# ScalarE loads the projection, TensorE multiplies zeros meanwhile, GpSimd copies the query maxima, and a new order table

## The chip, the cores and the metric

The kernel runs on one core of a Trainium2 chip. A core has five engines that run side by side, each through its own list of instructions in order: TensorE (PE, matrix products), VectorE (DVE), ScalarE (ACT), GpSimd (POOL) and SyncE (SP, which here only issues DMA transfers). The metric is the device time of one launch in microseconds; a kernel's time is the median of its runs.

## The reference

Two stages follow each other. The first is a linear attention with positive features for 8 batches and 8 heads of 576 tokens with 64 values each; the second is a feed-forward layer with a cosine gate.

```
def phi(x):                                        # 64 -> 256 features
    proj = einsum('bhsd,df->bhsf', x, w_phi)       # w_phi: 64 x 128
    proj = proj - max(abs(proj), axis=-1)
    return concatenate([exp(proj), exp(-proj)])
kv  = einsum('bhsf,bhsd->bhfd', phi(k), v);  z = sum(phi(k), axis=2)
out = (phi(q) @ kv) / (phi(q) @ z + 1e-6)          # -> x, 4608 tokens x 512
h = x @ w_in;  g = h * cos(h);  y = g @ w_out      # 512 -> 2048 -> 512
```

## The kernel before

The attention goes by 32 units of two heads each (`attention(u)`, L427). A unit's queries are projected by `q_mm` (L451) in two halves with the features on the partitions, copied out by ScalarE (`q_copy`, L457), and reduced to the largest absolute value over 128 features in three moves on VectorE: `q_red` (L464) reduces inside quarters of 32 partitions, `q_max` (L470) takes the maximum of the four quarters and writes it into each of the four (L474 once, L476 four times), `q_turn` (L478) transposes it so that GpSimd can subtract it (`q_sub`, L482). Keys are projected by `k_mm` (k_mm and a small k_end) with the tokens on the partitions; `k_max` takes their maxima on VectorE, and for the first eight units `k_sub` subtracts them by a matmul. ScalarE's `exp_k` and `exp_q` follow, then `kv_mm`, `z_mm` and `n_mm` on TensorE, the division (`invert`, `spread`, `turn`, `times`) and the store to `xs`.

The feed-forward layer goes by chunks of 512 tokens and by 16 tiles of the hidden width; `course` lists 15 visits of a chunk to some of the tiles (`visit(v)`). A visit runs `mm1`, a cosine on ScalarE and VectorE, and `mm2` (written as four steps "one" for a visit's first tile). The weights arrive as 64-bit words and are converted once (`convert(ft)`, L353): for the first four tiles GpSimd does three of the moves (`w.rest`, `w.low`, `w.add`), for the others VectorE.

Every piece of work is a `Step` with an engine, a cost, what it depends on and the buffers that it takes; the steps are numbered in the order in which the code makes them. The order in which they are issued is not computed: the table `ORDER` (L86) lists all 2888 numbers. An engine's instruction list is the table cut down to that engine's steps, so a late step holds up all that stands behind it on its engine. `plan()` (L240) walks the table, keeps a clock from the written costs, and gives each step that takes a bank of PSUM the bank that this clock says is free first.

Before all steps stand the constants: SyncE issues `w_phi` twice into the halves of `wphi` (L309), which all projections read; GpSimd writes small constants. The matrix products have four array shapes: full (mm1, mm2, one, k_sub, k_end), upper (q_mm, k_mm: 64 rows), left (kv_mm, n_mm: 64 columns) and quarter (z_mm: 32 columns).

Of the kernel before, what the change touches and what calls it, by code (L numbers as in the profile page):

```python
# [25 lines left out]
def phi_attention_then_cos_ffn(ctx: ExitStack, tc: tile.TileContext, qT, kT, vS, vT, w_phi, w_in, w_out, out):  # L26
# [41 lines left out]
    class Step:  # L68
# [15 lines left out]
    SWITCH = dict(e=1.3, s=1.3, full=0.21, left=0.145, quarter=0.12, upper=0.2)  # L84
    SHAPE = dict(mm1="full", mm2="full", one="full", k_mm="upper", k_end="full", t_mm="upper", t_end="full", s_mm="full", k_sub="full", kv_mm="left", n_mm="left", z_mm="quarter", q_mm="upper")
    ORDER = [  # L86
# [151 lines left out]
    LATENCY = dict(PE=0.35, ACT=0.25, DVE=0.2, POOL=0.25, SP=2.2)  # L238

    def plan():  # L240
        free = dict.fromkeys(LATENCY, 0.0)
        free["port"] = 0.0
        table = {}
        last = {}
# [702 lines left out]
```

## Time and profile before

| | us |
|---|---|
| median of 3 runs (lowest, highest) | 1092.85 (1092.62, 1094.83) |
| profiled execution | 1094.05 |
| its span in the trace | 1092.3 |
| TensorE busy / its weight loads | 1075.4 / 827.7 |
| VectorE busy | 725.2 |
| ScalarE busy | 717.2 |
| GpSimd busy | 127.3 |

Times inside a trace count from the start of its span. An engine's busy time leaves out the instructions of its sequencer. Matmuls are pipelined: each shows longer than the distance to its successor.

### The profile page before, as it was taken

The page shows a single profiled execution, that of the slowest core. Times are in us where ns is not written, and L with a number is a line of the kernel's source. Part 1 is how long each engine was busy: PE and PEld are TensorE (multiplying, and loading weights), DVE is VectorE, ACT ScalarE, POOL GpSimd, SP SyncE. Part 2 cuts the span into 40 slices and gives each one's busy share as a digit, 9 for nine tenths or more (in the row PEclk, how much of TensorE's full clock was granted, in tenths as well). Part 3 has the DMA queues.
Part 4 walks back from the last instruction along what each step waited for, and adds up shares of the span by engine and source line. Part 5 has one row for each costly group of instructions (what it writes and reads, how often), then busy time and mean ns, then how long its engine had stood idle before and what let it go on. Part 6 is the DMA issues. An engine that isn't in the chain of part 4 may idle for free.

```text
span 1092.3 us, 19509 instructions
## 1 busy us (share of the span) xinstructions
PE 1075.4 (98%) x7664; PEld 827.7 (76%) x7664; DVE 725.2 (66%) x1298; ACT 717.2 (66%) x1386; POOL 127.3 (12%) x91
## 2 busy tenths in 40 slices
PE   7999999999999999999999999999999999999998
PEld 4656666778888887788677787787777778888886
DVE  5899999989889868555577366773665354343432
ACT  5888889977666587657567666857667654443533
POOL 2654221000000011101031011110111000000000
PEclk9999999999999999999999999999999999999999
DMA  6564664356667355555241651345211620630441
GB/s 193 150 192 121 193 193 142 97 167 208 224 203 242 109 196 159 195 180 222 55 149 69 205 185 46 106 176 192 93 61 61 250 99 2 222 125 20 146 191 48
DMA packets 92603, 160.71 MB, mean 147 GB/s; under 512 B 43744, under 2 KB 52064, under 8 KB 84320
## 3 DMA queue, kind: packets, MB, share of 16 engines
q1 hardware_dynamic: 92512, 159.48, 43.9%
q8 instruction: 60, 0.98, 0.4%
q14 instruction: 31, 0.25, 0.1%
HBM read 117.51 MB, written 41.94 MB: 146 GB/s over the span
## 4 chain that ended last, share of the span: by engine, by line
PE 86%; DVE 6%; issue 0%; DMA 0%; ACT 0%; DVEq 0%
PE bank L798 35%; PE bank L832 12%; PE bank L833 12%; PE bank L834 12%; PE bank L691 4%; PE bank L642 4%; PE bank L681 2%; PE bank L455 2%; PE bank L493 2%; PE bank L648 1%; PE bank L568 0%; DVE g_c__1102 L809 0%; DMA out<-o_last 0%; DVE m_u__975 L466 0%; DVE g_c__1972 L809 0%
## 5 line engine op out<-in xcount | busy, mean ns | idle before, releaser
L813 ACT ACT_TABLE_LOAD x22 | 28.2, 1283 | 0.4
L484 POOL TENSOR_TENSOR pq_u__3673<-pq_u__3673,bq_u__4170 128x576 f32<-128x576 f32 x2 | 3.6, 1796 | 186.1 <-DVE bq_u__4170 L480 186.1
L872 DVE TENSOR_TENSOR o<-bank,o 128x512 f32<-128x512 f32 x24 | 16.2, 679 | 0.7 <-DMA o<-sums 0.5
L881 DVE COPY o<-bank 128x512 f32<-128x512 f32 x16 | 10.8, 677 | 5.9 <-PE bank L834 4.7
L603 ACT ACT_TABLE_LOAD x11 | 14.1, 1283 | 0.2
L879 ACT ACTIVATE o<-bank 128x512 f32<-128x512 f32 x16 | 9.5, 593 | 5.5 <-PE bank L834 5.5
L598 ACT ACT_TABLE_LOAD x10 | 12.8, 1283 | 0.2
L798 PE MATMUL bank<-xh_c__7472,w 128*128 128x512 f32 x32 | 12.8, 400 | 0.0
L798 PE MATMUL bank<-xh_c__6688,w 128*128 128x512 f32 x32 | 12.8, 399 | 0.0
L798 PE MATMUL bank<-xh_c__5272,w 128*128 128x512 f32 x32 | 12.8, 399 | 0.0
L798 PE MATMUL bank<-xh_c__4458,w 128*128 128x512 f32 x32 | 12.7, 396 | 0.0
L798 PE MATMUL bank<-xh_c__7041,w 128*128 128x512 f32 x32 | 12.5, 390 | 0.0
L798 PE MATMUL bank<-xh_c__5868,w 128*128 128x512 f32 x32 | 12.5, 390 | 0.0
L798 PE MATMUL bank<-xh_c__8219,w 128*128 128x512 f32 x32 | 12.5, 390 | 0.0
L798 PE MATMUL bank<-xh_c__5790,w 128*128 128x512 f32 x32 | 12.5, 390 | 0.0
L798 PE MATMUL bank<-xh_c__7889,w 128*128 128x512 f32 x32 | 12.5, 390 | 0.0
L798 PE MATMUL bank<-xh_c__6645,w 128*128 128x512 f32 x32 | 12.5, 390 | 0.0
L798 PE MATMUL bank<-xh_c__5941,w 128*128 128x512 f32 x32 | 12.5, 390 | 0.0
L798 PE MATMUL bank<-xh_c__4514,w 128*128 128x512 f32 x32 | 12.5, 390 | 0.0
L798 PE MATMUL bank<-xh_c__4696,w 128*128 128x512 f32 x32 | 12.5, 390 | 0.0
L798 PE MATMUL bank<-xh_c__7074,w 128*128 128x512 f32 x32 | 12.5, 390 | 0.0
L798 PE MATMUL bank<-xh_c__8223,w 128*128 128x512 f32 x32 | 12.5, 390 | 0.0
(3837 smaller groups left out, 4061.7 us busy)
## 6 DMA issues: line engine op xcount, KB each, us to landing
w<-w_parts SPq DMA_DIRECT2D x48, 1024.0 KB, 5.0
w_parts<-w SPq DMA_DIRECT2D x16, 1024.0 KB, 5.5
vmain<-vS SPq DMA_DIRECT2D x32, 256.0 KB, 4.7
out<-o SPq DMA_DIRECT2D x32, 256.0 KB, 3.0
sums<-o SPq DMA_DIRECT2D x24, 256.0 KB, 3.3
o<-sums SPq DMA_DIRECT2D x24, 256.0 KB, 3.2
vtail<-vT SPq DMA_DIRECT2D x64, 16.0 KB, 3.7
out<-o_last SPq DMA_DIRECT2D x4, 256.0 KB, 2.0
```

Of the source, the lines that this page charges most:

```text
L455: PE.matmul(out=ps[j], lhsT=wphi[r, :], rhs=d["qr"][r, hf * HALF:(hf + 1) * HALF], start=True, stop=True)
L493: PE.matmul(out=ps[j][:, P * s:P * s + P], lhsT=x[r, P * s:P * s + P], rhs=wphi[r, :], start=(s == 0), stop=w, skip_group_check=True)
L603: ACT.activation(out=e[:, s, :], in_=d["pq"][:, j * S:(j + 1) * S], func=AF.Exp, scale=1.0 - 2.0 * s)
L642: PE.matmul(out=acc[c:c + 64, n, i, :], lhsT=e[:, s, P * n + c:P * n + c + 64], rhs=vmain[u % 2][:, s, i, :], start=(s == 0 and i == 0 and ...
L681: PE.matmul(out=ps[32 * g:32 * g + 32], lhsT=d["z"][:, 2 * n + j, :], rhs=d["eq", j][:, n, hf * HALF:(hf + 1) * HALF], start=(n == 0), sto ...
L691: PE.matmul(out=d["nps", hf][64 * j:64 * j + 64], lhsT=d["kv"][:, 2 * n + j, :], rhs=d["eq", j][:, n, cut[hf]], start=(n == 0 and hf == 0) ...
L798: PE.matmul(out=h, lhsT=a[:, cs], rhs=d[b, kt], start=(k == 0), stop=(k == 3 * KT - 1))
L813: ACT.activation(out=m["g"], in_=m["g"], func=AF.Sin, bias=halfpi, scale=1.0)
L832: PE.matmul(out=a, lhsT=gh[:, t], rhs=w[:, 0], start=first, stop=False)
L833: PE.matmul(out=a, lhsT=gh[:, t], rhs=w[:, 1], start=False, stop=False)
L834: PE.matmul(out=a, lhsT=gl[:, t], rhs=w[:, 0], start=False, stop=last)
L872: DVE.tensor_tensor(out=o, in0=bank(acc[tb]), in1=o, op=ALU.add)
```

## The change

ScalarE's queue issues the two loads of `wphi`. VectorE writes a 128x128 tile of zeros, and TensorE multiplies it with itself seven times into bank 7 ahead of all steps. `q_max` writes the maxima into the first quarter only, and a new step `q_spread` copies them to the other three on GpSimd; `q_turn` depends on it. `plan()` no longer keeps a clock: a step gets the bank whose last user stands earliest in the table. The table is a new one, for 2920 steps (one more per unit). The written costs and latencies also differ, but in the new kernel nothing reads them any more.

```diff
     ORDER = [
-        0, 41, 2, 5, 3, 6, 7, 4, 8, 10, 11, 43, 46, 16, 57, 9, 12, 1192, 18, 20, 13, 44, 45, 48, 61, 19, 17, 58, 21,
...
-        2724, 2819, 2823, 2824, 2825, 2830, 2838, 2839, 2831, 2811, 2832, 2833, 2845, 2803, 2812, 2826, 2840, 2820,
...
+        2914, 2916, 2918, 2917, 2915, 2919,
     ]
...
     def plan():
-        free = dict.fromkeys(LATENCY, 0.0)
...
+        place = {steps[x]: i for i, x in enumerate(ORDER)}
+        owner = [None] * len(banks)
+
+        def last(b):
+            return -1 if b is None else max(place[v] for v in b.users)
 
         for x in (steps[i] for i in ORDER):
...
             for b in x.take:
                 if b.ring == "bank":
-                    at, b.slot = empty(x.eng)
+                    b.slot = min(range(len(banks)), key=lambda i: last(owner[i]))
+                    assert last(owner[b.slot]) < place[x]
                     owner[b.slot] = b
...
     for j in range(2):
-        SP.dma_start(out=wphi[64 * j:64 * j + 64, :], in_=w_phi)
+        ACT.dma_start(out=wphi[64 * j:64 * j + 64, :], in_=w_phi)
     halfpi = const.tile([P, 1], F32, name="halfpi")
     POOL.memset(halfpi, PI_2)
+
+    warm = const.tile([P, P], F32, name="warm")
+    DVE.memset(warm, 0.0)
...
+    WARM = 7
...
             DVE.tensor_tensor(out=m2, in0=m1[0:64], in1=m1[64:128], op=ALU.max)
-            for i in range(4):
-                DVE.tensor_tensor(out=m3[32 * i:32 * i + 32], in0=m2[0:32], in1=m2[32:64], op=ALU.max)
+            DVE.tensor_tensor(out=m3[0:32], in0=m2[0:32], in1=m2[32:64], op=ALU.max)
+
+        def q_spread():
+            m3 = d["m3"]
+            for i in range(1, 4):
+                POOL.tensor_copy(out=m3[32 * i:32 * i + 32], in_=m3[0:32])
...
-            qm = Step("DVE", 0.94, q_max, reds, take=[b["bq"]], use=[b["pq"]], port=True, kind=phase + "q_max")
-            qm = Step("DVE", 1.4, q_turn, [qm], use=[b["bq"]], kind=phase + "q_turn")
+            qm = Step("DVE", 0.41, q_max, reds, take=[b["bq"]], use=[b["pq"]], port=True, kind=phase + "q_max")
+            qm = Step("POOL", 0.45, q_spread, [qm], use=[b["bq"]], port=True, kind=phase + "q_spread")
+            qm = Step("DVE", 1.3, q_turn, [qm], use=[b["bq"]], kind=phase + "q_turn")
...
     with tc.manual_schedule(engines={ENG.PE, ENG.Activation, ENG.DVE, ENG.Pool, ENG.SP}):
+        for _ in range(WARM):
+            PE.matmul(out=banks[7][:, 0:P], lhsT=warm, rhs=warm, start=True, stop=True, skip_group_check=True)
         for x in plan():
             x.fn()
```

Cut down to TensorE's steps (a number is the unit, or with v the visit), the two tables begin like this:

```
before: q_mm0 x2, q_mm1 x2, k_mm0, k_mm1, k_sub0, k_end0, k_end1, k_sub0, k_sub1 x2, k_sub0, kv_mm0 x3, k_end2, k_sub1, k_mm2, ...
after:  k_mm0, q_mm0 x2, q_mm1 x2, k_sub0, k_end0, k_sub0, k_end1, k_sub0, k_mm1, kv_mm0 x3, k_sub1 x3, k_mm2, q_mm2, z_mm0, ...
```

SyncE's list begins with load0, load1, w.load0, load_v0, load2, load3, w.load1 before, and with load0, load1, load_v0, w.load0, load2, load_v1, load3 after.

## Rows read from the trace of the kernel before

**Rows 1.** The page's slices: busy tenths of 40 equal parts of the span.

```profile
PE   7999999999999999999999999999999999999998
...
DVE  5899999989889868555577366773665354343432
```

**Rows 2.** Stretches: length, busy us (and instructions) by engine, clock, DMA share, GB/s.

```profile
12.80:200.00 187.20, 181.16 (x2066) 118.77 (x2063) 175.43 (x349) 160.15 (x354) 72.79 (x42) 1.00 0.52 160
200.00:1080.00 880.00, 879.97 (x5534) 697.86 (x5534) 544.79 (x938) 551.50 (x1023) 53.13 (x34) 1.00 0.42 144
```

**Rows 3.** TensorE's waits from 12.8 to 200 us: total, times, longest; nine rows.

```profile
PE bank L590 <- DVE mk_u__293 L580: 1.6, 1, 1.6
...
PE bank L455 <- DVE pk_u__1718 L585: 0.2, 1, 0.2
```

**Rows 4.** Timeline of TensorE: start, length, instruction; the fourth visit's first matmul.

```profile
239.75 0.39 PE L798 MATMUL bank<-xh_c__2680,w 128*128 128x512 f32 x1
```

**Rows 5.** The chain that ended last: start, length, what; around 262 and 570 us.

```profile
261.68 5.44 PE bank L798 x24
...
562.72 5.47 PE bank L798 x24
568.19 1.11 PE bank L681 x16
569.29 2.10 PE bank L691 x16
571.39 1.87 PE bank L642 x64
...
573.71 0.69 PE bank L455 x4
574.39 0.89 PE bank L493 x16
575.28 0.49 PE bank L455 x4
```

**Rows 6.** Timeline of the first 14 us, with idle time before and its releaser.

```profile
0.81 1.21 SPq L309 DMA_DIRECT2D wphi<-w_phi  x2
...
1.68 0.52 POOL L325 MEMSET vtail<- 64x1 f32 x4
...
5.27 2.29 PE L455 MATMUL bank<-qr_u__117,wphi 64*128 64x288 f32 x8 [5.27 <-DMA qr_u__117<-qT]
...
7.05 0.48 DVE L466 TRANSPOSE_TENSOR_REDUCE m_u__129<-pq_u__130 128x9 f32<-128x288 f32 x1 [7.05 <-ACT pq_u__130 L462]
...
10.75 1.92 PE L493 MATMUL bank<-wphi,kr_u__118 64*128 64x128 f32 x16
...
12.46 1.20 PE L493 MATMUL bank<-wphi,kr_u__122 64*128 64x128 f32 x16
...
12.70 0.69 DVE L580 TENSOR_REDUCE mk_u__169<-bank 128x4 f32<-128x512 f32 x1 [2.38 <-PE bank L493]
```

**Rows 7.** DMA issues of the first 14 us: median us from issue to landing.

```profile
kr_u__118<-kT SPq DMA_DIRECT2D x1, 320.0 KB, 3.4
...
qr_u__121<-qT SPq DMA_DIRECT2D x1, 288.0 KB, 5.5
```

**Rows 8.** Line L476: ns min/median/max, first and last start; units 0, 1 and 5.

```profile
L476 DVE TENSOR_TENSOR m_u__160<-m_u__159 x4: 184/186/189, 9.5 to 10.1; 32x36 f32<-32x36 f32 x4
L476 DVE TENSOR_TENSOR m_u__287<-m_u__286 x4: 185/186/2285, 21.1 to 23.9; 32x36 f32<-32x36 f32 x4
...
L476 DVE TENSOR_TENSOR m_u__946<-m_u__945 x4: 185/188/2458, 72.7 to 75.6; 32x36 f32<-32x36 f32 x4
```

**Rows 9.** Timeline of VectorE and GpSimd near 15 and 46 us.

```profile
13.90 1.37 DVE L480 STREAM_TRANSPOSE bq_u__173<-m_u__160 128x1152 f32<-128x1152 f32 x1
...
15.45 2.76 POOL L484 TENSOR_TENSOR pq_u__130<-pq_u__130,bq_u__173 128x576 f32<-128x576 f32 x2 [13.26 <-ACT ek_u__198 L598]
...
46.28 2.37 POOL L54 TENSOR_TENSOR w_t_f__476<-w_t_f__476,w 128x1024 f32<-128x1024 f32 x1
```

More of the change, by code (lines that the diff above doesn't have):

```diff
@@ L81, in __init__ @@
             steps.append(self)
-    SWITCH = dict(e=1.3, s=1.3, full=0.21, left=0.145, quarter=0.12, upper=0.2)
+    SWITCH = dict(e=1.3, s=1.3, full=0.23, left=0.147, quarter=0.138, upper=0.195)
     SHAPE = dict(mm1="full", mm2="full", one="full", k_mm="upper", k_end="full", t_mm="upper", t_end="full", s_mm="full", k_sub="full", kv_mm="left", n_mm="left", z_mm="quarter", q_mm="upper")
     ORDER = [
[150 rows of a table removed]
[152 rows of a table added]
     ]
@@ L240, in plan @@
     def plan():
-        free = dict.fromkeys(LATENCY, 0.0)
-        free["port"] = 0.0
-        table = {}
-        last = {}
-        owner = [None] * 8
-        def end_of(v, eng):
-            return v.start + v.cost + (0.0 if v.eng == eng == "PE" else v.lat)
-        def empty(eng):
-            found = []
-            for i, b in enumerate(owner):
-                users = b.users if b is not None else []
-                if all(v.start is not None for v in users):
-                    found.append((max([0.0] + [end_of(v, eng) for v in users]), i))
-            return min(found)
+        place = {steps[x]: i for i, x in enumerate(ORDER)}
+        owner = [None] * len(banks)
+        def last(b):
+            return -1 if b is None else max(place[v] for v in b.users)
         for x in (steps[i] for i in ORDER):
-            t = max(free[x.eng], free["port"]) if x.port else free[x.eng]
-            for d in x.deps:
-                t = max(t, end_of(d, x.eng))
             for b in x.take:
                 if b.ring == "bank":
-                    at, b.slot = empty(x.eng)
+                    b.slot = min(range(len(banks)), key=lambda i: last(owner[i]))
+                    assert last(owner[b.slot]) < place[x]
                     owner[b.slot] = b
-                    t = max(t, at)
-                    continue
-                held = last.setdefault(b.ring, [])
-                if len(held) >= rings[b.ring]:
-                    t = max([t] + [end_of(v, x.eng) for v in held[-rings[b.ring]].users])
-                held.append(b)
-            if x.table not in (None, table.get(x.eng)):
-                x.cost += SWITCH[x.table]
-                table[x.eng] = x.table
-            x.start = t
-            free[x.eng] = t + x.cost
-            if x.port:
-                free["port"] = t + x.cost
         return [steps[i] for i in ORDER]
@@ L356, in convert @@
         slot = w_slot[ft] = Buf("w")
-        name, eng, cost = ("POOL", POOL, 2.4) if ft in W_POOL else ("DVE", DVE, 1.22)
+        name, eng, cost = ("POOL", POOL, 2.4) if ft in W_POOL else ("DVE", DVE, 1.135)
         def load():
@@ L399, in convert @@
         s1 = Step("SP", 3.2, load, take=[raw], kind="w.load")
-        s2 = Step("ACT", 2.1, scale, [s1], take=[t], use=[raw], kind="w.scale")
-        s3 = Step("DVE", 2.55, bits, [s2], use=[t, raw], port=True, kind="w.bits")
-        s4 = Step("ACT", 1.05, high, [s3], take=[slot], use=[t], kind="w.high")
+        s2 = Step("ACT", 2.05, scale, [s1], take=[t], use=[raw], kind="w.scale")
+        s3 = Step("DVE", 2.6, bits, [s2], use=[t, raw], port=True, kind="w.bits")
+        s4 = Step("ACT", 0.95, high, [s3], take=[slot], use=[t], kind="w.high")
         s5 = Step(name, cost, rest, [s3], use=[t], port=True, kind="w.rest")
@@ L443, in load_v @@
                 SP.dma_start(out=vtail[u % 2][64 * j:64 * j + 64, j, 0:64], in_=vT[u][j])
-        ld = Step("SP", 1.9, load, take=[b["kr"], b["qr"]], kind=phase + "load")
-        lv = Step("SP", 0.9, load_v, [chain_v.get(u - 1)], take=[b["v"]], kind=phase + "load_v")
+        ld = Step("SP", 3.0 if u < 4 else 2.3, load, take=[b["kr"], b["qr"]], kind=phase + "load")
+        lv = Step("SP", 0.9, load_v, [chain_v.get(u - 1)], take=[b["v"]], lat=3.2, kind=phase + "load_v")
         chain_v[u] = lv
@@ L609, in attention @@
             d["kb", i] = kb[i]
-        main = Step("PE", 0.88, lambda: k_mm(0), [ld], take=kb[:2] + pks[:2], use=[b["kr"]], kind=phase + "k_mm")
-        tail = Step("PE", 0.22, lambda: k_mm(1), [ld], take=[kb[2], pks[2]], use=[b["kr"]], kind=phase + "k_end")
+        main = Step("PE", 0.89, lambda: k_mm(0), [ld], take=kb[:2] + pks[:2], use=[b["kr"]], kind=phase + "k_mm")
+        tail = Step("PE", 0.14, lambda: k_mm(1), [ld], take=[kb[2], pks[2]], use=[b["kr"]], kind=phase + "k_end")
         for i in range(3):
-            cost = (1.3 if i < 2 else 0.55) if u not in K_SUMS else 0.67 if i < 2 else 0.28
+            cost = (1.32 if i < 2 else 0.51) if u not in K_SUMS else 0.6 if i < 2 else 0.21
             kms.append(Step("DVE", cost, lambda i=i: k_max(i), [tail if i == 2 else main], use=[kb[i], pks[i]],
@@ L621, in attention @@
             e = Buf("ek" if i < 2 else "ek_t")
-            eks.append(Step("ACT", 1.06 if i < 2 else 0.42, lambda i=i: exp_k(i), [kms[i]] + gate, take=[e], use=[pks[i]] + ([kb[i]] if u in K_SUMS else []),
+            eks.append(Step("ACT", 1.045 if i < 2 else 0.4, lambda i=i: exp_k(i), [kms[i]] + gate, take=[e], use=[pks[i]] + ([kb[i]] if u in K_SUMS else []),
                             table="e", kind=phase + "exp_k"))
@@ L626, in attention @@
             e = Buf("eq")
-            eqs.append(Step("ACT", 1.16 if u not in Q_SUMS else 1.75, lambda j=j: (s_exp if u in Q_SUMS else exp_q)(j),
+            eqs.append(Step("ACT", 1.15 if u not in Q_SUMS else 1.75, lambda j=j: (s_exp if u in Q_SUMS else exp_q)(j),
                             ([sm] if u in Q_SUMS else [qs[j]]) + gate, take=[e], use=[sb_[j], sb_[2]] if u in Q_SUMS else [b["pq"]],
@@ L667, in attention @@
                         kind=phase + "kv_mm")
-        ko = Step("ACT", 0.6, kv_out, [last], use=[acc, b["kv"]], kind=phase + "kv_out")
+        ko = Step("ACT", 0.45, kv_out, [last], use=[acc, b["kv"]], kind=phase + "kv_out")
         N0 = CT
@@ L725, in attention @@
         dv = Step("ACT", 0.9, spread, [dv], use=[b["rb"]], kind=phase + "spread")
-        dv = Step("DVE", 0.78, turn, [dv], use=[b["rb"]], kind=phase + "turn")
+        dv = Step("DVE", 0.7, turn, [dv], use=[b["rb"]], kind=phase + "turn")
         mm = Step("PE", 1.94, n_mm, [zm], take=[nps], use=[zps, b["kv"]] + eqb, kind=phase + "n_mm")
-        outs = [Step("DVE", 0.69 if ps is nps else 0.22, lambda hf=hf: times(hf), [mm, dv], use=[ps, b["rb"]], kind=phase + "times") for hf, ps in ((1, zps), (0, nps))]
+        outs = [Step("DVE", 0.61 if ps is nps else 0.14, lambda hf=hf: times(hf), [mm, dv], use=[ps, b["rb"]], kind=phase + "times") for hf, ps in ((1, zps), (0, nps))]
         stored[u] = Step("SP", 0.9, store, outs, use=[b["rb"]], kind=phase + "store")
@@ L778, in visit @@
             h = Step("ACT", 0.53, high, loads[kt] if v == 0 else [loads[kt]], take=[x], use=[rawb[kt]], kind=stage + "x_high")
-            ks.append(Step("DVE", 0.68, low, [h], use=[x, rawb[kt]], port=True, kind=stage + "x_low"))
+            ks.append(Step("DVE", 0.61, low, [h], use=[x, rawb[kt]], port=True, kind=stage + "x_low"))
             xb.append(x)
@@ L840, in visit @@
             chain["mm1"] = [s1]
-            s2 = Step("ACT", 1.18, copy, [s1], take=[g], use=[ps, hs], kind=stage + "copy")
-            s3 = Step("DVE", 0.74, reduce, [s2], use=[g, hs], port=True, kind=stage + "reduce")
+            s2 = Step("ACT", 1.0, copy, [s1], take=[g], use=[ps, hs], kind=stage + "copy")
+            s3 = Step("DVE", 0.61, reduce, [s2], use=[g, hs], port=True, kind=stage + "reduce")
             s4 = Step("ACT", 0.62, cosine, [s3], use=[g], table="s", kind=stage + "cosine")
-            s5 = Step("DVE", 0.66, times, [s4], use=[g, hs], port=True, kind=stage + "times")
+            s5 = Step("DVE", 0.61, times, [s4], use=[g, hs], port=True, kind=stage + "times")
             s6 = Step("ACT", 0.53, high, [s5], take=[gh], use=[g], kind=stage + "high")
-            s7 = Step("DVE", 0.68, low, [s6], take=[gl], use=[g, gh], port=True, kind=stage + "low")
+            s7 = Step("DVE", 0.61, low, [s6], take=[gl], use=[g, gh], port=True, kind=stage + "low")
             if first or last and v == len(course) - 1:
@@ L891, in visit @@
                 old = [Step("SP", 0.9, fetch, [partial[c, tb], begun], take=[o], kind=stage + "fetch")]
-            cp = Step(eng, 0.6 if eng == "ACT" else 0.68, out_copy, [done[tb] if v == len(course) - 1 else before] + old, take=[] if old else [o],
+            cp = Step(eng, 0.5 if eng == "ACT" else 0.61, out_copy, [done[tb] if v == len(course) - 1 else before] + old, take=[] if old else [o],
                       use=[acc[tb]] + ([o] if old else []), kind=stage + "out_copy")
```

4 lines of the change are left out of this document (2 added, 2 removed), and 299 rows, old and new, of the table ORDER.

## The prediction

> **What bounds the kernel now.** I began with the page's busy shares and its 40 slices [rows 1]. The reader is to see two things: TensorE is busy in nearly every tenth from the second slice on, and VectorE is just as full in the first seven or eight slices (some 200 us) and only there. The table of stretches makes that exact [rows 2]. From 200 to 1080 us TensorE idles for 0.03 us and VectorE has slack (545 of 880 us). From 12.8 to 200 us TensorE idles 6.0 us (187.20 - 181.16) while VectorE is busy 175.4 of 187.2 us, 94%. So the late part is TensorE's own work, and the early part is a race of TensorE and VectorE. The view of waits for that early stretch says who is late [rows 3]: nine waits, 5.9 us in all, and every one but a ScalarE wait of 0.4 us ends at a VectorE instruction.
>
> The idle time understates the loss, because a matmul whose successor starts late still counts as busy through its pipeline. So I made an account up to one place, the first matmul of the fourth visit, at 239.75 us [rows 4]. Ahead of it the old table puts 30 q_mm at 0.49 us, 16 k_mm at 0.89, 15 kv_mm groups at 2.32 (from 571.39 to 573.71), 15 z_mm at about 1.0 (1.11 less the change of shape that follows it), 15 n_mm at about 2.0 (2.10 likewise), 25 mm1 or mm2 at 2.72 (half of 5.44) and 12 "one" at a quarter of that, 0.68 [rows 5]. 16 large k_sub, 8 small ones and 15 k_end have no row of their own at full pace; I estimate them from their columns as one k_mm and as a quarter of one. The sum is 14.7 + 14.2 + 34.8 + 15 + 30 + 68 + 8.2 + 14.2 + 5.1 = 204 us. The place is reached 234.5 us after the first matmul at 5.27 [rows 6]. So 30 us are lost there, and they are all that can be had outside the start and the switches of later stretches.
>
> **The start (wphi on ScalarE's queue, zeros multiplied, k_mm first).** SyncE now spends 1.21 us issuing wphi before it can issue the first query load [rows 6]. On ScalarE's queue those two issues cost SyncE nothing, and ScalarE has nothing to copy before the first matmul of 5.27 us [rows 6], so they are hidden; if ScalarE's table load (1.28 us) went first, wphi would land 1.3 us later, near 5 us, when keys come too. The loads move up by 1.2 us. The new table starts TensorE with k_mm of unit 0, so it waits for the first key load and not the query load: issued one slot behind the query load, at some 1.4 us (0.81 + 0.6, half of wphi's two issues), and 3.4 us from issue to landing [rows 7], it is there at 4.8 us, 0.4 us ahead of the first matmul now.
>
> The first 16 matmuls of L493 take 1.92 us and the next 16 take 1.20 us [rows 6]: the clock rose from its 1.2 to its 2.4 GHz level near 12.7 us, in the middle of work (the granted-clock column shows 1.00 in all these rows, so I go by the lengths). Seven products with zeros start near 1 us and are as many columns as seven of L493's sixteen pairs of records; at the low level, one behind the other and not two beside each other, I estimate 3 us for them (7 x 2 x 0.21, from 1.92 us for eight pairs of matmuls). If they raise the clock before the keys land, k_mm is done after 0.9 us and not 1.9. Between gain of nothing and 1.0 us for the chain I take half, 0.5.
>
> What matters more is VectorE. It now starts at 7.05, does unit 0's query reductions and then sits idle 2.38 us until k_mm delivers at 12.70 [rows 6]. In the new order k_max of unit 0 comes first, near 6.5 us, with the query reductions ready behind it. I take 2.4 us for that idle time and 0.5 us for the clock: **-2.9 us**. Bounds: 0 (the second query load lands 5.5 us after issue [rows 7] and holds q_mm of unit 1 as now) and -4.2 (the 7.19 us from the first matmul to 12.46 [rows 6] hold 3.0 us of matmul work at full clock).
>
> **The query maxima.** Four L476 instructions follow each other from 9.5 to 10.1 us, each 0.186 us long [rows 8]; three fewer, with the 0.03 us between them, free 0.66 us per unit. 15 units come before 239.75 us: 15 x 0.66 = -9.9 us of VectorE's time. In three of those units (1, 3 and 5) one of the four took 2.29 to 2.46 us and not 0.19 [rows 8]: it stood until GpSimd's weight instruction, 2.37 us long, was over [rows 9]. That is 3 x 2.1 = 6.3 us more, which may go, or may meet the next two-operand instruction of VectorE; I take nothing for it.
>
> In return VectorE's q_turn now waits for GpSimd: a step over to GpSimd of 0.18 us (13.90 + 1.37 to 15.45 [rows 9]), three copies, a step back. The trace has no such copy. Its nearest rows are the GpSimd memsets of a 64x1 column, 0.13 us each [rows 6], and, above, q_sub at 1.38 us for 128x576 [rows 9]; three copies of 32x36 lie between 0.4 and 4.1 us, far nearer the low end (a sixteenth of q_sub's columns). I take 0.5, and 0.9 for the round trip. The new table puts other VectorE steps between q_max and q_turn in most units, but none for units 2, 4 and 7: 3 x 0.9 = +2.7. The copies of units 2, 4, 5 and 6 stand in GpSimd's queue behind a weight instruction of 2.37 us; I take one such wait: +2.4. Who waits for them: all of VectorE's queue, then q_sub, exp_q, z_mm. Net **-4.8 us** (bounds -16.2, with the blocks gone, and +9.6, with all seven waits of the slower rival).
>
> A rule bears on this. The trace shows the block: an L476 of 2.29 us that elsewhere takes 0.19, with GpSimd's instruction over it [rows 8, 9]. The Trainium skill, page "GPSIMD Engine Reference", section "1. Specifications", says that GpSimd's SBUF interface is shared with VectorE, with contention where VectorE has two SBUF inputs. By the rule the two-input instructions of a unit's q_max fall from five to two, but the copies enter the same contest.
>
> **The order table.** I numbered the steps as the code makes them (one new step per unit, 2920) and read both tables for TensorE. The work is the same 600 steps; the changes of matmul shape from one step to the next fall from 180 to 157, 19 to 22 of them early. A change costs between 0.03 us (two mm1 with a change behind them 5.47, without 5.44) and 0.20 (a q_mm behind one 0.69, else 0.49) [rows 5]; I take 0.11. Early: 20 x 0.11 = 2.2, of which I take half, 1.1, since where VectorE is late TensorE's saving is idle time. Late: 4 x 0.11 = 0.4. ScalarE's table loads go from 44 to 46, +2.6 us, all behind that place, where ScalarE has slack. On SyncE's queue the first value load is put ahead of the first weight load, and the second and later query and key loads go ahead of the first stores; these stores are read by the second visit only, so I cost that at nothing; without that cover a store late by one load costs some 3 us. Of the bank choice by place I can't say more than that the banks are as many; it is in the next term. The order also removes or adds single waits; I take -1.1 for them, from the 5.9 us of [rows 3], since the new table puts VectorE's k_max and q_red closer in step with TensorE; bounds -5.9 and +5.9. The late 880 us keep their work and, but for 0.4 us, their time.
>
> **Sum.** -2.9 - 4.8 - 1.1 - 0.4 - 1.1 = -10.3 us. The profiled execution took 1094.05 us with a span of 1092.3; it would take 1083.75. It stood 1.2 us above the median of the runs, 1092.85, so I predict 1092.85 - 10.3 = **1082.5 us**.
>
> **Rivals.** (1) *More than that:* freed VectorE time also removes the handing back and forth; VectorE's blocks (6.3) and a quarter more of the waits (1.4) go as well: -18, 1075 us. For it: 30 us are lost before 239.75 us, and VectorE's early share is 94%. Against it: ScalarE is busy 160 of the 187 us [rows 2] and becomes the next bound. (2) *Only the start and the switches:* q_turn's wait for GpSimd gives back what VectorE gained, and the clock stays low: -2.4 - 1.5 = -3.9, 1089 us. Speaks for it that three units have nothing between q_max and q_turn. (3) *Slower:* GpSimd's queue becomes the bound. The copies of units 2, 4, 5 and 6 stand behind one or two weight instructions each, seven in all: 7 x 2.4 = 16.8 us of VectorE standing in order before some 80 us, in place of the 2.4 counted, and units 0, 1, 8, 10 and 13, with one VectorE step between, lose 0.9 each: 4.5. It decides from 12.7 us of such waits on; at 21.3 the time is 1092.85 - 10.3 - 2.4 + 21.3 = 1101 us. Against it: now GpSimd's queue has gaps (72.8 us busy of 187 [rows 2]). (4) *Nothing happens:* the loads, not TensorE, set the start, and new waits in VectorE's queue cancel the rest: 1092 us.
>
> **Chances.** A change within 0.2% (2.2 us) can't be told from none. Forecast, 1077.5 to 1088: 0.50. Rival 1, below 1077.5: 0.20. Rival 2, 1088 to 1090.6: 0.13. Rival 4, 1090.6 to 1095: 0.08. Rival 3, above 1095: 0.09. So faster 0.83, same 0.08, slower 0.09. For 8 in 10 the range reaches from 1073 to 1091; the forecast's own is 1077.5 to 1088.
>
> **What would show it.** Start: first real matmul near 4.8 us, L493's sixteen in 1.2 us or less, no VectorE gap of 2.4 us before 13 us. Maxima: one L476 per unit, three GpSimd copies near 0.15 us each, and the wait of q_turn for them below 1 us. Order: the fourth visit's first matmul near 230 us and the same length from there to the end. I am wrong if that place stands past 237 us, if VectorE waits for GpSimd by more than 8 us in sum, or if the time behind the place changes by over 3 us.

## The result, and the profile after

| | before | after |
|---|---|---|
| median of 4 runs (lowest, highest), us | 1093.59 (1092.62, 1094.83) | 1081.46 (1080.87, 1083.35) |
| profiled execution / its span, us | 1094.05 / 1092.3 | 1081.44 / 1079.7 |
| VectorE / ScalarE / GpSimd busy, us | 725.2 / 717.2 / 127.3 | 711.8 / 720.8 / 157.6 |

The ratio is 0.9896 (95% interval 0.9881 to 0.9912): the kernel is 12.1 us faster, and 1082.5 was forecast. The sum came out; its terms didn't, and they missed in opposite directions.

The slices and the two stretches of the changed kernel (columns as in [rows 2]) stand first. Its lines have other numbers: L476 is k_mm, L434 q_mm, L564 k_max, L574 k_sub, L454 the second maximum of `q_max` (it writes the first quarter), L459 the copies, L463 `q_turn`, L782 mm1.

```profile
PE   9999999999999999999999999999999999999998
...
DVE  6899999988898877645667456764564353434333
```

```profile
12.80:200.00 187.20, 183.35 (x2149) 125.91 (x2144) 174.70 (x316) 166.51 (x363) 84.89 (x84) 1.00 0.51 157
200.00:1067.00 867.00, 867.00 (x5422) 689.64 (x5421) 529.83 (x873) 545.82 (x1009) 70.60 (x85) 1.00 0.43 146
```

Early on TensorE idles 3.85 us where it idled 6.0 [rows 2], and it does 83 more matmuls in the same 187 us. VectorE is as busy as before (174.7 of 187.2): the freed time went into earlier work. Late, TensorE has no idle time, as before. TensorE's waits from 12.8 to 200 us (total, times, longest) answer to [rows 3]:

```profile
PE bank L574 <- DVE mk_u__945 L564: 0.8, 1, 0.8
PE bank L574 <- DVE mk_u__915 L564: 0.8, 1, 0.8
PE bank L574 <- DVE mk_u__938 L564: 0.7, 1, 0.7
PE bank L574 <- DVE mk_u__750 L564: 0.7, 1, 0.7
PE bank L665 <- ACT eq_u__1248 L587: 0.4, 1, 0.4
PE bank L434 <- DVE pk_u__1437 L569: 0.3, 1, 0.3
```

Four of the six are k_sub waiting for k_max; the longest of before, 1.6 us, is gone. The place where the prediction counted up to, the fourth visit's first matmul, is here in the timeline of TensorE (start, length, instruction):

```profile
227.59 0.39 PE L782 MATMUL bank<-xh_c__2542,w 128*128 128x512 f32 x1
```

It stood at 239.75 [rows 4]: the place comes 12.16 us earlier. From it to the end of the span it was 852.55 us and is 852.11.

The start, as the timeline shows it (start, length, instruction, in brackets the idle time and its releaser), answers to [rows 6]:

```profile
0.81 1.19 ACTq L284 DMA_DIRECT2D wphi<-w_phi  x2
...
1.13 3.22 PE L887 MATMUL bank<-warm 128*128 128x128 f32 x14 [1.13 <-DVE warm L289]
...
1.27 0.41 SPq L417 DMA_DIRECT2D kr_u__127<-kT  x1
...
5.13 0.46 PE L476 MATMUL bank<-wphi,kr_u__127 64*128 64x128 f32 x2 [0.78 <-DMA kr_u__127<-kT]
...
5.78 1.04 PE L476 MATMUL bank<-wphi,kr_u__127 64*128 64x128 f32 x13 [0.20 <-DMA wphi<-w_phi]
...
6.77 0.69 DVE L564 TENSOR_REDUCE mk_u__162<-bank 128x4 f32<-128x512 f32 x1 [5.69 <-PE bank L476]
6.78 1.13 PE L434 MATMUL bank<-qr_u__126,wphi 64*128 64x288 f32 x7
...
11.19 1.38 DVE L463 STREAM_TRANSPOSE bq_u__240<-m_u__171 128x1152 f32<-128x1152 f32 x1 [0.70 <-POOL m_u__171 L459]
```

The first key load is issued at 1.27 us and its matmuls begin at 5.13. The second half of `wphi` lands 0.6 us later, at 5.78, and k_mm breaks off for it. After that k_mm and q_mm run at full pace: the clock records of the trace put its rise at 4.08 us, where before they put it at 12.76. VectorE starts at 6.77, and the gap of 2.38 us is gone.

The copies (line, engine, tile, count: ns min/median/max, first and last start), and VectorE's waits for them up to the fourth visit:

```profile
L459 POOL COPY m_u__171<-m_u__171 x3: 204/206/208, 10.4 to 10.9; 32x36 f32<-32x36 f32 x3
...
L459 POOL COPY m_u__263<-m_u__263 x3: 685/733/1221, 16.0 to 18.0; 32x36 f32<-32x36 f32 x3
L459 POOL COPY m_u__480<-m_u__480 x3: 205/206/210, 30.0 to 30.5; 32x36 f32<-32x36 f32 x3
```

```profile
DVE bq_u__486 L463 <- POOL m_u__480 L459: 0.9, 1, 0.9
DVE bq_u__1259 L463 <- POOL m_u__1253 L459: 0.9, 1, 0.9
DVE bq_u__775 L463 <- POOL m_u__769 L459: 0.9, 1, 0.9
DVE bq_u__240 L463 <- POOL m_u__171 L459: 0.7, 1, 0.7
```

A copy takes 0.206 us, three with their gaps 0.7, and four units wait, 3.4 us in all. The blocks of [rows 8, 9] did not go away; the one L454 that now stands under a weight instruction takes 2.34 us:

```profile
77.60 2.41 POOL L366 TENSOR_TENSOR w_t_f__1049<-w_t_f__1049,w_t_f__1047 128x1024 f32<-128x1024 f32 x1 [4.14 <-ACT d_u__1080 L692]
77.72 2.34 DVE L454 TENSOR_TENSOR m_u__1100<-m_u__1099 32x36 f32<-32x36 f32 x1
```

To weigh all of them I summed, over VectorE's instructions ahead of the fourth visit, what each took beyond the median of its own form where that is over 0.15 us. This sum, called "blocks" below, is 16.2 us before and 15.8 after. VectorE's idle time up to that place, summed over the gaps before its instructions, fell from 24.3 to 20.5 us.

### The profile page after: what moved, and what is told of

Same layout as the page of the kernel before. It is cut to its first block, busy times and chain, and to the rows that moved or that the text cites. A ratio compares the mean times of both kernels' runs of the same rounds, so it can differ in the third digit from the quotient of the medians.

```text
span 1079.7 us, 19604 instructions
## 1 busy us (share of the span) xinstructions
PE 1069.3 (99%) x7678; PEld 830.6 (77%) x7678; DVE 711.8 (66%) x1203; ACT 720.8 (67%) x1388; POOL 157.6 (15%) x187
## 4 chain that ended last, share of the span: by engine, by line
PE 87%; DVE 5%; issue 0%; DMA 0%; POOL 0%; ACT 0%; DVEq 0%; POOLq 0%
PE bank L782 36%; PE bank L816 12%; PE bank L818 12%; PE bank L817 12%; PE bank L675 4%; PE bank L626 4%; PE bank L665 2%; PE bank L434 2%; PE bank L476 2%; PE bank L632 1%; PE bank L552 1%; DMA out<-o_last 0%; DVE g_c__1300 L793 0%; DVE g_c__1130 L800 0%; DVE m_u__1584 L445 0%
## 5 line engine op out<-in xcount | busy, mean ns | idle before, releaser
L459 POOL COPY m_u__4056<-m_u__4056 32x36 f32<-32x36 f32 x3 | 1.6, 540 | 174.4 <-DVE m_u__4056 L454 174.3
L782 PE MATMUL bank<-xh_c__6319,w 128*128 128x512 f32 x32 | 12.9, 402 | 0.0
L782 PE MATMUL bank<-xh_c__5560,w 128*128 128x512 f32 x32 | 12.7, 398 | 0.0
L782 PE MATMUL bank<-xh_c__7588,w 128*128 128x512 f32 x32 | 12.7, 396 | 0.0
L782 PE MATMUL bank<-xh_c__4428,w 128*128 128x512 f32 x32 | 12.6, 393 | 0.0
L782 PE MATMUL bank<-xh_c__6921,w 128*128 128x512 f32 x32 | 12.5, 391 | 0.0
L782 PE MATMUL bank<-xh_c__6769,w 128*128 128x512 f32 x32 | 12.5, 390 | 0.0
L782 PE MATMUL bank<-xh_c__5807,w 128*128 128x512 f32 x32 | 12.5, 390 | 0.0
L782 PE MATMUL bank<-xh_c__7130,w 128*128 128x512 f32 x32 | 12.5, 390 | 0.0
L782 PE MATMUL bank<-xh_c__5878,w 128*128 128x512 f32 x32 | 12.5, 390 | 0.0
L782 PE MATMUL bank<-xh_c__7977,w 128*128 128x512 f32 x32 | 12.5, 390 | 0.0
L782 PE MATMUL bank<-xh_c__5928,w 128*128 128x512 f32 x32 | 12.5, 390 | 0.0
L782 PE MATMUL bank<-xh_c__8059,w 128*128 128x512 f32 x32 | 12.5, 390 | 0.0
L782 PE MATMUL bank<-xh_c__4632,w 128*128 128x512 f32 x32 | 12.5, 389 | 0.0
L782 PE MATMUL bank<-xh_c__8100,w 128*128 128x512 f32 x32 | 12.5, 389 | 0.0
L782 PE MATMUL bank<-xh_c__4557,w 128*128 128x512 f32 x32 | 12.5, 389 | 0.0
L782 PE MATMUL bank<-xh_c__4759,w 128*128 128x512 f32 x32 | 12.4, 389 | 0.0
```

The costliest lines, as they stand in the source:

```text
L782: PE.matmul(out=h, lhsT=a[:, cs], rhs=d[b, kt], start=(k == 0), stop=(k == 3 * KT - 1))
```

## The experiments

A time is made of three stretches, read from each trace's timeline: from the start of the span to the first z_mm, from there to the fourth visit's first matmul, and from there to the end of the span. The stretches are those of one execution, the median is that of all runs; the last stretch is good to 0.05 us only, as it ends with a span read to a tenth. The middle stretch repeats to within 0.05 us between the changed kernel and those that differ from it only at the start (e8 to e11), and before and e3 differ by 0.14, so it is the sharpest measure here. "Clock rise" is where the clock records first show the 2.4 GHz level.

| kernel | median us | ratio to before [95%] | clock rise | to first z_mm | to fourth visit | to the end |
|---|---|---|---|---|---|---|
| before | 1093.59 | | 12.76 | 24.86 | 214.89 | 852.55 |
| after | 1081.46 | 0.9896 [0.9881, 0.9912] | 4.08 | 18.67 | 208.92 | 852.11 |
| e1 max on VectorE | 1095.5 | 1.0015 [1.0005, 1.0024] | 9.05 | 20.10 | 222.41 | 852.09 |
| e2 old order | 1094.36 | 1.0 [0.9988, 1.0012] | 3.99 | 19.76 | 215.69 | 853.95 |
| e3 start only | 1092.72 | 0.9985 [0.9976, 0.9995] | 4.81 | 22.64 | 214.75 | 852.61 |
| e4 copies only | 1085.29 | 0.9916 [0.9901, 0.9931] | 9.85 | 21.29 | 209.59 | 852.62 |
| e5 banks only | 1106.15 | 1.0113 [1.0096, 1.0129] | 9.75 | 23.97 | 227.31 | 854.02 |
| e6 start and copies | 1085.02 | 0.9924 [0.9909, 0.9939] | 9.59 | 21.11 | 209.65 | 852.64 |
| e7 after, old banks | 1084.68 | 0.9922 [0.9907, 0.9937] | 10.55 | 20.70 | 208.95 | 852.85 |
| e8 no zeros | 1083.09 | 0.991 [0.9896, 0.9925] | 8.93 | 20.30 | 208.89 | 852.11 |
| e9 wphi on two queues | 1083.48 | 0.9904 [0.9885, 0.9922] | 8.79 | 20.11 | 208.91 | 852.18 |
| e10 ten zeros | 1081.88 | 0.9891 [0.987, 0.9911] | 6.17 | 19.43 | 208.90 | 852.17 |
| e11 wphi on SyncE | 1083.23 | 0.9904 [0.9881, 0.9928] | 5.12 | 19.25 | 208.87 | 852.18 |
| e12 no wait for copies | 1082.41 | 0.9897 [0.9881, 0.9914] | 10.13 | 20.47 | 208.54 | 852.19 |

**e1: the changed kernel without GpSimd's copies.** VectorE writes all four quarters, `q_spread` is empty.

```diff
-            DVE.tensor_tensor(out=m3[0:32], in0=m2[0:32], in1=m2[32:64], op=ALU.max)
+            for i in range(4):
+                DVE.tensor_tensor(out=m3[32 * i:32 * i + 32], in0=m2[0:32], in1=m2[32:64], op=ALU.max)
...
         def q_spread():
+            return
```

> The changed kernel with one part undone: VectorE writes the query maxima into all four quarters again, and the new step on GpSimd does nothing; order table, banks, zeros and the loads of wphi stay. Theory (the freed VectorE time is worth 4.8 us net): the kernel before times 0.9896 plus about 5 us, 1086 to 1089 us, and the first matmul of the fourth visit moves from 227.6 to about 232 to 235 us. Rival A (the order holds the gain, who copies does not matter): within 1.5 us of the changed kernel, 1080 to 1083 us. Rival B (the old blocks of 2.3 us come back too, all of VectorE's time counts): 16 us more, about 1097 us.

It took 1095.5 us, 14 above the changed kernel and nearest to rival B: without the copies this table has no gain left. 13.5 us of it lie between the first z_mm and the fourth visit. The blocks rise from 15.8 to 22.2 us. Unit 6 (and 5) shows where, by the line that writes the quarters:

```profile
L455 DVE TENSOR_TENSOR m_u__769<-m_u__768 x4: 184/186/189, 55.9 to 56.5; 32x36 f32<-32x36 f32 x4
L455 DVE TENSOR_TENSOR m_u__942<-m_u__941 x4: 184/188/2456, 68.6 to 71.5; 32x36 f32<-32x36 f32 x4
L455 DVE TENSOR_TENSOR m_u__1100<-m_u__1099 x4: 187/2324/2330, 84.6 to 89.6; 32x36 f32<-32x36 f32 x4
```

Three of unit 6's four stood 2.3 us each, one behind the other. TensorE's longest wait, for a k_max that VectorE reaches only behind unit 5's four, is 3.9 us (total, times, longest):

```profile
PE bank L573 <- DVE mk_u__948 L563: 3.9, 1, 3.9
```

And TensorE fell back to its lower clock twice, at 70.5 to 77.3 and 94.4 to 101.2 us; the first shows in the stretch from 66 to 80 us (columns as in [rows 2]), with 9.33 of 14 us busy and a granted clock of 0.76:

```profile
66.00:80.00 14.00, 9.33 (x50) 4.61 (x52) 11.84 (x21) 5.62 (x14) 7.72 (x5) 0.76 0.23 74
```

Counted on VectorE, the 14 us are work (15 x 0.66 = 9.9) and blocks (+6.4), which lie in part beside each other. Counted on TensorE, the 13.5 us of the middle stretch are 6.2 us more of idle time (10.07 against 3.85) and 7.3 us more of busy time. In that stretch it is busy for 11.1 us at the lower level; I estimate that half of it, 5.6 us, is what the clock costs. That is no accident of one execution: all ten runs show a granted clock of 0.993 or 0.994, the four of the changed kernel 1.000.

**e2: the changed kernel with the old order.** Start, copies and banks stay; the table is that of before, with each `q_spread` right behind its `q_max`.

> The changed kernel with the old order table, with each unit's new GpSimd step put right behind its q_max; the rest of the change stays (wphi on ScalarE's queue, zeros, copies on GpSimd, banks by place). Theory (start about 2 us without k_mm first, copies 4.8): 1084 to 1088 us, 180 changes of matmul shape. Rival A (the order holds the gain): 1090 to 1094 us. Rival B (GpSimd's queue is late under a table that did not foresee it): above 1094 us, VectorE idle before q_turn by more than 10 us in sum.

1094.36 us: no gain over before. This looked as if the order carried everything. The row in the table is that of the fastest of its ten runs, 1091.24 us; they reach up to 1095.7, and the slower ones show a granted clock down to 0.994 where this one shows 1.000. The waits of TensorE (total, times, longest) told of something else:

```profile
PE bank L625 <- ACT hs_c__2047 L788: 3.3, 1, 3.3
PE bank L781 <- DVE pk_u__1067 L568: 2.1, 1, 2.1
```

Neither is among [rows 3] in that size: mm1 waits for VectorE's subtraction in k_max, which reads a bank, and kv_mm for ScalarE's copy of an mm1 out of a bank. These look like waits for a bank to come free, and the bank choice by place was part of this kernel.

**e3: before with the new start only** (wphi on ScalarE's queue, seven products of zeros).

```diff
-        SP.dma_start(out=wphi[64 * j:64 * j + 64, :], in_=w_phi)
+        ACT.dma_start(out=wphi[64 * j:64 * j + 64, :], in_=w_phi)
...
+        for _ in range(7):
+            PE.matmul(out=banks[7][:, 0:P], lhsT=warm, rhs=warm, start=True, stop=True, skip_group_check=True)
```

> The kernel before with the start alone changed: wphi on ScalarE's queue and seven products of zeros; order, banks and maxima as before. Theory: the loads come 1.2 us earlier and the clock is up before the first query matmul, but VectorE still waits for the keys' projection, which now stands at full clock: 2 to 3.5 us faster, 1089.5 to 1091.5 us. Rival A (VectorE's later work takes it back): no change, 1092 to 1094 us. Rival B (wphi lands later behind the large loads and eats what the queue gained): 0.5 to 1.5 us faster.

-1.3 us by the medians, as rival B has it. In its profiled execution, the fastest of its ten, the clock rose at 4.81 us and the first z_mm came 2.22 us earlier than before; what lies behind is unchanged (214.75, 852.61).

**e4: before with the copies only**: one maximum and three copies, everything else old.

> The kernel before with the maxima alone changed: one VectorE instruction and three GpSimd copies per unit, each new step right behind its q_max in the old table. Theory: VectorE has 9.9 us less to do before 240 us and gives back about 5 in waits for GpSimd: 1086 to 1090 us. Rival A (VectorE stands idle for GpSimd at every q_turn, as the old table puts nothing between, so that nothing is won): 1091 to 1095 us. Rival B (head of GpSimd's queue): above 1095 us.

-8.7 us, a little more than the theory's best. The middle stretch falls by 5.30 us. The first z_mm comes 3.57 us earlier; 1.85 us of that stand already at the first kv_mm (18.04 to 16.19), but there e5, without any copies, has 16.28, so this part is put down to the start's own spread between executions. The other 1.7 us fit the block of 2.1 us in unit 1 [rows 8], which is gone. That leaves 7.0 us by the trace and 8.7 by the medians. All the waits of TensorE from 12.8 to 240 us are these three, against nine of 5.9 us [rows 3]:

```profile
PE bank L648 <- ACT pq_u__1579 L463: 0.4, 1, 0.4
PE bank L840 <- DVE gl_c__1488 L54: 0.3, 1, 0.3
PE bank L456 <- DVE pk_u__1718 L591: 0.2, 1, 0.2
```

Here the blocks did fall, by 8.9 us (16.2 to 7.3), beside the 9.9 of work. VectorE's idle time rose by 8.2 (24.3 to 32.5). So of 18.8 us that VectorE was spared 7 to 8.7 shortened the kernel, and no run says how much of that is work and how much blocks.

**e5: before with the bank choice by place only.**

```diff
-                    at, b.slot = empty(x.eng)
+                    b.slot = min(range(len(banks)), key=lambda i: last(owner[i]))
```

> The kernel before with the choice of banks alone changed: by place in the table in place of the clock kept from costs; 119 of 524 bank takes then follow another user. Theory (formed from the two waits of 2.3 and 3.4 us that the old table showed together with the rest of the change, at the first mm1 and at kv_mm of unit 11): 3 to 7 us slower, 1097 to 1101 us. Rival (the start or the copies made these waits, not the banks): within 2 us of the kernel before.

12.7 us slower, well beyond the theory's 3 to 7. In the old table the choice by place puts the same two waits into the way as in e2, here 3.5 and 3.3 us, and the clock falls four times; from 80 to 95 us TensorE is granted 0.77:

```profile
PE bank L771 <- DVE pk_u__1058 L558: 3.5, 1, 3.5
PE bank L615 <- ACT hs_c__2038 L778: 3.3, 1, 3.3
```

```profile
80.00:95.00 15.00, 11.49 (x78) 8.55 (x76) 10.77 (x18) 8.67 (x18) 8.61 (x5) 0.77 0.12 34
```

In the middle stretch, 12.4 us longer than that of before, TensorE is idle for 5.8 us more (10.2 against 4.4) and busy for 6.6 us more; for 15.3 us it is busy at the lower level. So not the order but the banks, chosen for another table, ate e2's gain; e6 shows it directly.

**e6: start and copies, old table, old banks** (e3 and e4 together).

> The kernel before with the start and the copies changed, old table, old choice of banks. Theory (the parts add up and the earlier result under the old table was lost to the banks): 8.7 + 1.3 us, 1083 to 1085 us; the rest to the changed kernel, 2 to 3 us, is then the new table with its banks. Rival (the two parts get in each other's way): 1089 to 1094 us.

1085.02 us. It has the same table as e2 and differs from it only in the choice of banks: 9.3 us faster by the medians, 6.0 by the two traces, neither of which has a fall of the clock in it. Against e4 it is 0.3 us faster, but set against the runs of before taken beside each, e6 gains 8.5 us and e4 8.7. Behind the copies the new start brought nothing that can be measured in this kernel; the first matmul moved up 1.28 us (5.70 to 4.42), the first z_mm by 0.18. In its profiled execution the clock rose only at 9.59 us, in spite of the zeros.

**e7: the changed kernel with the old bank choice** (the clock of written costs in `plan()`, as before, but fed with the new kernel's costs).

> The changed kernel with the old choice of banks (a clock kept from the new costs); 82 of 524 bank takes then follow another user. Theory (the new table was made for banks by place; by a clock from measured costs the banks are as good): within 1.5 us of the changed kernel, 1080 to 1083 us. Rival A (the table needs its banks): 3 to 6 us slower. Rival B (place is the worse rule for any table): 2 to 4 us faster.

1084.68 us, 3.2 above the changed kernel. By the median alone the banks would be worth 3 us, as rival A has it. The trace doesn't bear that out: 2.03 us are there at the first z_mm already, with the clock rising at 10.55 us, 0.03 lie in the middle stretch, and 0.74 behind the last matmul, where the last copy out waits longer for the store ahead of it (1.78 us, after 1.41). Part of the rest is the clock again: its two slower runs show 0.996, the two faster 1.000. Against e6 (same start, same kind of banks, late clock) the new table wins 0.3 us by the median, 0.9 by the span.

**e8: the changed kernel without zeros** (`WARM = 0`).

> The changed kernel without the seven products of zeros. The clock then rises some microseconds after the first real matmul and not at 4.1 us. Theory: the first k_mm and the query projections run at the low level, k_mm is done 0.9 us later and VectorE starts 0.9 us later: 0.5 to 2 us slower, 1082 to 1083.5 us. Rival A (the loads set the pace of the start): no change, 1081 to 1082 us. [...]

1083.09 us, 1.63 above the changed kernel. The first z_mm is 1.63 later, the fourth visit 1.60: all of it is at the start, with a clock that rises at 8.93 us, as the theory has it.

**e9: the two halves of wphi on two queues**, the first on SyncE, the second on ScalarE.

```diff
-        ACT.dma_start(out=wphi[64 * j:64 * j + 64, :], in_=w_phi)
+        (SP, ACT)[j].dma_start(out=wphi[64 * j:64 * j + 64, :], in_=w_phi)
```

> The changed kernel, with the first half of wphi issued by SyncE ahead of all loads and the second half by ScalarE. In the changed kernel's trace the second half lands at 5.74 us, 0.61 us behind the first key load, and the first k_mm of unit 0 waits for it in its middle. Theory A (that wait is a cost of the move to ScalarE's queue): each half is first in its queue and both land before the first keys; SyncE's loads move back by one issue, 0.6 us; k_mm starts near 5.7 us and runs without a break, so z_mm of unit 0 starts where it did (18.7 us) or up to 0.6 us earlier, and the time is 0 to 0.6 us below the changed kernel. Rival (the halves share the DMA engines with whatever lies in the other queue, so the order of issue doesn't matter): the second half still lands behind the keys, the keys are 0.6 us later, and the time is 0.6 us above.

The wait is gone as theory A has it: k_mm starts at 5.76 us and runs its sixteen without a break, though at the low clock (row below). But the time is 2.0 us above the changed kernel, outside both. Its clock rose at 8.79 us. Against e8, which had no zeros and rose as late, it is 0.2 us early at the first z_mm; e7, with zeros and the rise at 10.55 us, is 0.4 us late.

```profile
5.76 2.08 PE L476 MATMUL bank<-wphi,kr_u__127 64*128 64x128 f32 x16 [1.27 <-DMA kr_u__127<-kT]
```

**e10: ten products of zeros** (`WARM = 10`).

> The changed kernel with ten products of zeros and not seven. With seven, the clock rose at 4.08 us in its profiled execution, but at 9.6 and 10.6 us in two other kernels with the same seven. Theory A (the zeros end too early to carry the clock over to the first keys in every execution): with ten they run on to 5 us, the clock has risen before 6 us in the profile, and the median falls by up to 0.7 us against the changed kernel. Rival (when the clock rises doesn't hang on three more products): the rise lies anywhere between 4 and 11 us, and the median is the same within 0.5 us; if the clock stays low the zeros end at 1.13 + 10 x 0.46 = 5.7 us, hold the first k_mm up by 0.6 us, and the median is up to 0.6 us above.

The rival: the clock stayed low through all twenty records, they end near 5.7 us and hold up the first k_mm, and the clock rose at 6.17 us.

```profile
1.13 4.63 PE L887 MATMUL bank<-warm 128*128 128x128 f32 x20 [1.13 <-DVE warm L289]
5.70 1.89 PE L476 MATMUL bank<-wphi,kr_u__130 64*128 64x128 f32 x15
```

The median, 1081.88 (1081.1 to 1084.1), can't be told from the changed kernel's.

**e11: the changed kernel with wphi on SyncE**, as before.

> The changed kernel with both halves of wphi issued by SyncE ahead of its loads, as in the kernel before; zeros, copies, table and banks as in the changed kernel. Theory A (as the prediction has it, SyncE's 1.2 us of issuing are on the path): the first keys land 1.2 us later, the first k_mm starts near 6.3 us, and z_mm of unit 0 starts 1.2 us later than in the changed kernel; the median is 1.2 us above. Rival (wphi's later landing on ScalarE's queue, 5.74 us, takes half of that back): wphi is there before the keys, k_mm runs without a break, and the time is 0.3 to 0.8 us above. If ScalarE's queue has no part in the start's gain at all: the same within 0.3 us.

The first k_mm starts at 6.30 us, 1.17 later, and needs 1.16 us for its sixteen without a break; the first z_mm is only 0.58 us later. That is the rival's number by the trace (the clock rose at 5.12 us). The median is 1.8 us higher, with runs from 1082.08 to 1084.79.

**e12: nobody waits for the copies.** `q_turn` reads the maxima of the four quarters apart; the kernel leaves the maximum across the quarters out of its result.

```diff
-            DVE.transpose(out=d["bq"], in_=d["m3"].unsqueeze(2).broadcast_to([P, 4 * NJ, 32]))
+            DVE.transpose(out=d["bq"], in_=d["m1"].unsqueeze(2).broadcast_to([P, 4 * NJ, 32]))
```

> The changed kernel with q_turn reading the maxima over four quarters apart (the input of q_max, same size) and not GpSimd's copies: the cross-quarter maximum is left out of the result, the copies still run and nobody waits for them. In the changed kernel VectorE waits 3.4 us for the copies in units 0, 2, 4 and 7. Theory A (VectorE is the bound up to the fourth visit, so its waits are on the path): that visit's first matmul comes 2.5 to 4 us earlier than in the changed kernel when both are set against their own z_mm of unit 0 or later by the share of unit 0 (0.7 us), and the median is 2.5 to 4 us below the changed kernel, near 1078 us. Rival (TensorE's own pace or the blocks of VectorE under GpSimd's weight instructions take the freed time): under 1 us at that visit, and the median is 1080.5 us or above. If the forecast's price had been paid (3 round trips and one wait in the queue, 5.1 us), the gain would be 5 us.

The 3.4 us of waits are gone, and the middle stretch is 0.38 us shorter, not 2.5 to 4. The clock fell once in it, from 68.2 to 71.6 us. These are TensorE's three longest waits up to the fourth visit, and the stretch around the fall:

```profile
PE bank L574 <- DVE mk_u__945 L564: 0.9, 1, 0.9
PE bank L574 <- DVE mk_u__938 L564: 0.7, 1, 0.7
PE bank L574 <- DVE mk_u__750 L564: 0.7, 1, 0.7
```

```profile
66.00:73.00 7.00, 6.08 (x32) 2.96 (x30) 5.29 (x10) 3.02 (x9) 6.01 (x7) 0.76 0.00 1
```

From z_mm of unit 3 to that of unit 4, where the fall lies, e12 takes 0.92 us longer than the changed kernel; without that it would have won 1.3. So VectorE's waits for the copies cost 0.4 to 1.3 us, and theory A falls: TensorE still waits for three of the four k_max that it waited for. No variant has a lower median than the changed kernel.

## Why the prediction was right, and where it wasn't

**The sum: partly luck.** The copies brought 2.2 to 3.9 us more than their -4.8. The start, the order and the banks together brought 1.7 to 2.1 us less than their -5.5: from e4 to the changed kernel it is 3.8 us by the medians, 3.4 with each set against its own runs of before.

**What bounds it: right.** The gain lies ahead of the fourth visit. "Near 230 us" was 227.59. It is less than half of the 30 us that the account found lost there. The time behind the place changed by -0.44 us, and -0.4 was forecast from four changes of shape, but that agreement is luck. Counted over the matmuls of the traces, only one change fewer stands there (88 before, 87 after), and the work on either side isn't the same: the new table puts one z_mm and one n_mm (32 matmuls, 3.0 us at the prediction's prices) behind the place and one mm2 (12 matmuls, 2.7 us) ahead of it. So some 0.3 of the 12.16 us are work moved and not time won.

**The query maxima: -4.8 forecast, -7.0 (trace) to -8.7 (median) measured in e4.** This is the mis-sized term. VectorE was spared the 9.9 us and, beside them, 8.9 us of blocks that were put at nothing; 7 to 8.7 us of the 18.8 came out of the kernel's time. The charge of +5.1 against them did not come in that size. Three round trips at 0.9 were foreseen, and four waits of 0.7 to 0.9 came, in units 0, 2, 4 and 7, so the rows were read rightly; but taking them all away (e12) gave 0.4 to 1.3 us, since TensorE went on waiting for three of its four k_max all the same. The wait at the head of GpSimd's queue, +2.4, did not come at all: the longest wait for copies is 0.9 us. Waits of VectorE were put on the path at their full length without asking who stands behind them.

**Blocks at nothing: right for the wrong reason.** In the old table the copies more than halve them (16.2 to 7.3). In the new table they stay at 15.8, on other instructions, as the prediction's "may meet the next two-operand instruction" had it; without the copies they would be 22.2 (e1). On the rule of the Trainium skill, page "GPSIMD Engine Reference", section "1. Specifications", that VectorE with two SBUF inputs contends with GpSimd: the trace agrees, the L455 of e1 taking 2.32 us in place of 0.186. Of the contest that the copies enter themselves the trace shows little: unit 1's three took 0.69 to 1.22 us, not 0.206.

**The start: -2.9 forecast; without k_mm first -1.3 (e3, median) and nothing measurable behind the copies (e6).** The 2.4 us for VectorE's gap were to come from k_mm standing first, which only the new table has; no run has that alone, so the whole term is measured only together with the order (above: 3.4 to 3.8 of 5.5). The parts were as described: keys at 5.13 us (4.8 forecast), no gap on VectorE, L493's sixteen (now L476) done 1.8 us after their start, with a break, not 1.2, for `wphi` came 0.6 us after the keys. Two things failed. SyncE's 1.2 us were counted as a gain, while ScalarE's queue delivers wphi later: of 1.17 us at the first matmul 0.58 are left at the first z_mm (e11). And the zeros raise the clock early only in some executions. The 0.5 us set for the clock are 1.6 where it rises early (after against e8), and where it doesn't, e9 is 0.2 us ahead of e8 and e7 0.4 behind it.

**The order and the banks: -2.6 forecast, -3.6 measured as e6 to after, but not for the reasons given.** With the clock late in both, the table, k_mm first with it, gives 0.3 to 0.9 us (e6 to e7). Of the rest, 3.2 us, the traces have 2.0 at the start, where the clock rises 6.5 us earlier. In the middle stretch the new table saves TensorE 3.4 us of busy time against e6 (208.5 to 205.1, some 0.3 of it work moved), but its idle time rises by 2.7 us (1.15 to 3.85). So the forecast was right that TensorE's saving turns into idle time where VectorE is late, and the half that it took off for this was too little. Its -1.1 for single waits went the other way: with the copies and the old table three waits of 0.9 us are left (e4, e6), and the new table has six of 3.7. That the banks were "as many", so with no price of its own, was a gap: chosen by place they cost 12.7 us in the old table and nothing on TensorE in the new. A choice of buffer belongs to the order that it was made for.

**The rivals.** Rival 1 asked for the blocks to go and for 2.5 us of TensorE's waits, the 1.1 in the sum and 1.4 on top. These waits fell by 2.2 us (5.9 to 3.7), but the blocks stayed. Rival 2's handing back didn't happen. Rival 3 needed 12.7 us of waits for GpSimd; 3.4 came. Rival 4's new waits in VectorE's queue are these same 3.4 us, worth 0.4 to 1.3.

Open: what k_mm first is worth by itself; how the gain of the copies divides between work and blocks; and what makes the clock rise early in one execution and late in another, and with that how much of the 3.2 us between e7 and the changed kernel is chance. Four runs of e7 reach down to 1083.81, and three of four of the changed kernel stand at 1081.5 or below.

## What to carry to other kernels

A wait on the busiest engine costs only what the engine behind it then waits for: follow it one step further before you price it. Time taken from an engine that sets the pace is worth only as much as the others then wait less, here 7 to 8.7 of 18.8 us. A rule that hands out buffers is to be tried with the order that it will serve: the same rule was worth nothing in one table and 12.7 us of loss in another.

## What the runs showed of the hardware that was not expected

Products of zeros (seven, in e10 ten) were followed by a rise of the clock anywhere from 3.99 to 10.55 us: in the ten profiled executions with zeros five rose by 6.2 us and five after 8.7; without zeros it was 8.93 to 12.76. In the new table the first z_mm follows it: 18.67 us with a rise at 4.08, 19.25 at 5.12, 19.43 at 6.17, 20.11 at 8.79, 20.70 at 10.55, so some 2 us in all (e9, e10 and e11 differ in their loads or zeros too), which nothing later gives back. The Trainium skill, page "TensorE: Matmul & The Clock Gate", section Part 1: The HAM clock gate (the "warmup" mystery), says that the moment of the rise varies from run to run, by about half a microsecond. The traces agree that it varies, but by 6.6 us here with zeros in front of the work; what decides it no run here shows.

The clock also fell in the middle of work, behind stalls of TensorE: twice in e1 (the first time inside the wait of 3.9 us), four times in e5, once in e12 for 3.4 us. In e12 two waits of 0.7 and 0.9 us for k_max stood ahead of it; the changed kernel has the same two, 0.7 and 0.8 us, and kept its clock.

A small load on a queue of its own isn't served first: wphi, issued at 0.81 us on ScalarE's queue, landed its halves at 4.31 and 5.74 us beside the large loads, and at 2.83 and 3.68 in the kernel before, where SyncE issued it ahead of them, at 0.81 us too.
